# Spectral mixing, dense experts and routed experts on one core: products that follow a short chain on VectorE or ScalarE issued one unit later

## The chip, the cores and the metric

The kernel runs on one core of a Trainium2 chip. The metric is the device time of one execution in microseconds; of several runs the median counts. Engines are named as the profile names them: PE is TensorE (PEld its weight loads), DVE is VectorE, ACT is ScalarE, POOL is GpSimd, SP is SyncE, which issues most DMAs. TensorE's clock has two levels here, 1.2 and 2.4 GHz; the profile's PEclk is the share that was granted, 1.00 for the higher level and 0.5 for the lower.

## The reference

Three stages follow each other. Eight sequences of 3072 tokens with 256 channels are taken to frequencies, mixed there by a complex 256 x 256 product with a bias, shrunk towards zero, and taken back. The second stage is a dense layer, the third sends each token to the best of eight experts, of which each takes its first 768 tokens.

```python
X = np.fft.rfft(x, axis=1)                      # x: 8 x 3072 x 256
Yr = Xr @ w_r - Xi @ w_i + b_r; Yi = Xr @ w_i + Xi @ w_r + b_i
Yr = sign(Yr) * max(abs(Yr) - 0.01, 0)          # Yi likewise
x = np.fft.irfft(Yr + 1j * Yi, n=3072, axis=1).reshape(24576, 256)
r = max(x @ w_in, 0); x = (s * r * r + b) @ w_out      # 256 -> 2048 -> 256
logits = x @ w_gate; e = argmax(logits)         # 8 experts
# a token is kept if fewer than 768 tokens before it chose e
out[i] = softmax(logits)[i, e] * (max(x[i] @ w1[e], 0) @ w2[e])   # 0 if not kept
```

## The kernel before

The program order of every engine is written out by hand. The main loop goes through 8 batches of 64 **units** each, 512 units in all; a batch is a sequence, and 8 units make a **tile** i of 384 tokens. A unit is `s_unit`: four products of 384 columns on PE (line 724) for two slices of the hidden layer, a Relu on ACT (L729) and a square on DVE (L730). The squares go to routing logits; the dense layer's own output is only computed for the tokens that can need it.

Behind `s_unit`, each unit issues in this order: what `slot[k]` holds for unit k; the logit transposes `lg_fin` that are due (list `fin`); one item of the queue `todo`; and `lg_set` and `lg_out`, when a tile's logits are due (list `pend`). The slots carry the transforms of the next batch: in units 1 to 16 the first transform (`f1_mm`, one product `pz` a unit, L225), in units 22 to 50 the groups (`g_a`, `g_b`, `g_c`: products `pf`, `pmx`, `pi1`), and in units 4 and 5 of each tile the inverse (`i2_mm`, L391, copied by ACT and turned by DVE, L407, in `i2_rows`). PE, DVE and ACT each take their instructions in this order, so a product whose operand isn't there yet holds up the products of all later units.

PSUM has eight banks: two pairs for `s_unit` (`hp`), one for logits (`lp`), and three (`bgp`, by `psum()`) that all other products share.

The places that the change touches:

- **`lg_set`, `lg_out`, `lg_fin`.** Three units behind a tile's last unit, 18 products form its logits in the bank `lg`, and ACT copies them to `ls` (L760). `lg_fin` turns `ls` with four PE transposes into `plt` (L768), and DVE adds up to `LG` (L771). It comes one unit behind the copy, 64 times less four: four tiles of batch 1 have it in the same unit.
- **`decide_items`**, once for each batch: on DVE, items a, c, d and e compare bounds of the logits and count the tokens that stay open; item f counts across partitions with two small products `prt` (L864), and eight items `to_list` write lists by indirect DMAs from POOL's queue (L878). For batch b from 2 on, the queue takes them in right behind the last `lg_fin` of the batch; for batches 0 and 1 they stand behind the items of the next two points. Batch 7 has its items in the tail.
- **`xroute_items`**, once in batch 1 from its unit 51 (M = 8), once in the tail (M = 4): exact softmax and ranks. Items a and b run on DVE and ACT, c ranks by two products `prt` (L1055, L1056), d splits the rank, c2 makes the gates, and for each pair of columns e builds one-hot tables (DVE, L1108 to L1115) and f multiplies them into `ptb` (L1122).
- **`bound_items`**, in batch 0 by slots, and a second time (`diff`) in the queue behind `xroute_items` and `flags`: a makes squares and sums of weights on DVE, b fills a tile of ones, adds up across partitions with `pnr` (L691), and takes roots on ACT. `lg_set` of batch 2, unit 10, needs what it makes.
- **`load_p2`**, in batch 7, units 4 to 26, an item in every second unit: weights are loaded into `cf` buffers, copied by ACT (L1158), split by DVE (L1159) and summed on POOL (`bc`, L1161 and L1164). Then comes an empty item, and g fills a tile of ones (L1170) and multiplies (`pbc`, L1171). The buffers of `cf` are later those of `sq`, the input of the dense layer for the exact tokens.

Of the kernel before, what the change touches and what calls it, by code (L numbers as in the profile page):

```python
# [10 lines left out]
F32 = mybir.dt.float32  # L11
# [8 lines left out]
C = 256  # L20
# [20 lines left out]
NKEY = 8  # L41
# [96 lines left out]
FIRST_LAG = 13  # L138
GRAM_TO = 10
XB_AT = (2, 3, 4, 5)  # L140
WARM_F1 = 18
WARM_GROUPS = 11
MOE_CONV_AT = (0, 0, 1, 2, 3, 3, 4, 5, 6, 6, 7, 7, 8)
# [6 lines left out]
class Kern:  # L150
# [501 lines left out]
    def bound_items(self, pp, diff=False):  # L652

        nc, V = self.nc, self.nc.vector
        wb, bet = (self.wogd, self.bed) if diff else (self.wogb, self.bet)

        def own():

            v = [pp.tile([128, k], F32, tag=f"ow{n}", name="ow") for n, k in enumerate((1, E, 1, E, 1, NF))]
            mx, pr, pm, oh, bf, tf = v  # L660
            V.tensor_reduce(out=mx, in_=self.cnt, axis=AX.X, op=ALU.max)
            V.scalar_tensor_tensor(out=pr, in0=self.cnt, scalar=mx, in1=self.e8, op0=ALU.is_ge, op1=ALU.mult)
            V.tensor_reduce(out=pm, in_=pr, axis=AX.X, op=ALU.max)
            V.tensor_scalar(out=oh, in0=pr, scalar1=pm, scalar2=None, op0=ALU.is_equal)
            V.tensor_tensor(out=pr, in0=self.bw, in1=oh, op=ALU.mult)
            V.tensor_reduce(out=bf, in_=pr, axis=AX.X, op=ALU.add)
            V.tensor_scalar(out=self.cd, in0=self.cn, scalar1=bf, scalar2=1e-5, op0=ALU.subtract, op1=ALU.add)
            x = self.tq
            V.tensor_tensor(out=x, in0=self.tw, in1=oh.unsqueeze(1).to_broadcast([128, NF, E]), op=ALU.mult)
            V.tensor_reduce(out=tf, in_=x, axis=AX.X, op=ALU.add)  # L670
            V.tensor_tensor(out=self.tw, in0=self.tw, in1=tf.unsqueeze(2).to_broadcast([128, NF, E]), op=ALU.subtract)

        def a():
            tw = self.wk.tile([128, 3, NF, E], F32, tag="cl", name="tw", bufs=1)
            self.tw, self.tq, t4 = tw[:, 0], tw[:, 1], tw[:, 2]
            V.tensor_scalar(out=self.tw, in0=self.wog[:, :, 0:E], scalar1=self.ws, scalar2=None, op0=ALU.mult)
            if diff:
                own()
            V.tensor_tensor(out=self.tq, in0=self.tw, in1=self.tw, op=ALU.mult)
            V.tensor_reduce(out=self.nrm[:, 2:3], in_=self.tq.rearrange("p f e -> p (f e)"), axis=AX.X, op=ALU.add)  # L680
            V.tensor_tensor(out=t4, in0=self.tq, in1=self.tq, op=ALU.mult)
            V.tensor_reduce(out=self.nrm[:, 3:4], in_=t4.rearrange("p f e -> p (f e)"), axis=AX.X, op=ALU.add)
            V.tensor_copy(out=wb[:, :, 0:E], in_=self.tw)
            V.tensor_tensor(out=wb[:, :, 16:16 + E], in0=self.tw, in1=wb[:, :, 0:E], op=ALU.subtract)
            V.scalar_tensor_tensor(out=self.tw, in0=self.tw, scalar=-1.0, in1=self.tw, op0=ALU.mult, op1=ALU.max)

        def b():
            ones = self.wk.tile([128, 128], F32, tag="t", name="ones4", bufs=3)
            V.memset(ones, 1.0)
            pb = self.psum("pnr")  # L690
            nc.tensor.matmul(pb[:, :4], ones, self.nrm, start=True, stop=True)  # L691
            n = [pp.tile([128, k], F32, tag=f"nr{m}{diff}", name="nr") for m, k in enumerate((4, 4, 1, 1, 1, 1))]
            one, two, v, eps, x, rho = n
            nc.scalar.activation(out=one, in_=pb[:, :4], func=AF.Sqrt)
            nc.scalar.activation(out=two, in_=one, func=AF.Sqrt)
            V.tensor_scalar(out=eps, in0=two[:, 0:1], scalar1=U12, scalar2=two[:, 1:2], op0=ALU.mult, op1=ALU.add)
            V.tensor_scalar(out=eps, in0=eps, scalar1=1.05, scalar2=1e-20, op0=ALU.mult, op1=ALU.max)
            V.tensor_tensor(out=x, in0=pb[:, 2:3], in1=one[:, 0:1], op=ALU.mult)
            V.tensor_scalar(out=x, in0=x, scalar1=15.0 / (E * 512.0 * FF), scalar2=1e-30, op0=ALU.mult, op1=ALU.max)
            nc.scalar.activation(out=v, in_=x, func=AF.Sqrt)  # L700
            V.reciprocal(out=rho, in_=v)
            V.tensor_tensor(out=rho, in0=rho, in1=eps, op=ALU.mult)
            V.reciprocal(out=x, in_=rho)
            V.tensor_tensor(out=x, in0=x, in1=two[:, 3:4], op=ALU.add)
            V.tensor_tensor(out=x, in0=x, in1=eps, op=ALU.mult)
            V.tensor_tensor(out=x, in0=x, in1=eps, op=ALU.mult)
            V.tensor_scalar(out=x, in0=x, scalar1=1.1, scalar2=None, op0=ALU.mult)
            V.tensor_copy(out=bet[:, E:2 * E], in_=x.to_broadcast([128, E]))
            V.tensor_scalar(out=rho, in0=rho, scalar1=1.05, scalar2=None, op0=ALU.mult)
            V.tensor_scalar(out=self.tq, in0=self.tq, scalar1=rho, scalar2=None, op0=ALU.mult)  # L710
            V.scalar_tensor_tensor(out=wb[:, :, E:2 * E], in0=self.tw, scalar=U8, in1=self.tq, op0=ALU.mult, op1=ALU.add)
        return [a, b]


    def s_unit(self, b, i, u):
# [102 lines left out]
    def decide_items(self, b):  # L818

        nc, V = self.nc, self.nc.vector  # L820
        v = {}
# [40 lines left out]
        def f():  # L862
# [9 lines left out]
            v["x"], v["c"] = t("x", [NKEY], I32), t("c", [NKEY], I32)  # L872
            V.scalar_tensor_tensor(out=v["x"], in0=self.i128[:N1, :NKEY], scalar=off, in1=x, op0=ALU.add, op1=ALU.add)
            V.tensor_scalar(out=v["c"], in0=v["k"], scalar1=-1.0, scalar2=float(KEY + NK * b), op0=ALU.mult, op1=ALU.add)  # L874
        return [a, c, d, e, f] + [lambda n=n: self.to_list(n, v["x"], v["c"]) for n in range(NKEY)]

    def to_list(self, n, x, c):
        self.nc.gpsimd.indirect_dma_start(  # L878
# [140 lines left out]
    def xroute_items(self, M, LG, hi, lo, blk, gates, valid=None):  # L1019

        nc, V = self.nc, self.nc.vector
        v = {}
# [77 lines left out]
        n = 2  # L1100
# [18 lines left out]
        def f(k):  # L1119
            ps = self.psum("ptb")  # L1120
            for m in range(n):
                nc.tensor.matmul(ps[:, :240], v["ol"][:, m], v["rh"][:, m].rearrange("p a c -> p (a c)"),  # L1122
                                 start=(m == 0), stop=(m == n - 1))
            tv = self.T.rearrange("p a c -> p (a c)")
            V.tensor_tensor(out=tv, in0=ps[:, :240], in1=tv, op=ALU.add)
        it = [a, b, c, d, c2]
        for k in range(M // n):
            it += [lambda k=k: e(k), lambda k=k: f(k)]
        return it

    def flags(self):
# [10 lines left out]
    def load_p2(self, p2):  # L1142

        nc = self.nc
        self.wo = p2.tile([128, 2, NF, C], F32R, tag="wo", name="wo")
        bc = p2.tile([128, C], F32, tag="bc", name="bc")
        st = {}

        def load(k):
            st[k] = self.p2c.tile([128, 512], F32, tag="sq", name="cf", bufs=3)  # L1150
            nc.sync.dma_start(out=st[k], in_=self.wd[k])

        def use(k):
            if k + 2 < 8:
                load(k + 2)
            s = slice(2 * k, 2 * k + 2)
            w = st.pop(k).rearrange("p (k c) -> p k c", k=2)
            nc.scalar.copy(out=self.wo[:, 0, s], in_=w)  # L1158
            nc.vector.tensor_tensor(out=self.wo[:, 1, s], in0=w, in1=self.wo[:, 0, s].bitcast(F32), op=ALU.subtract)  # L1159
            if k == 0:  # L1160
                nc.gpsimd.tensor_tensor(out=bc, in0=w[:, 0], in1=w[:, 1], op=ALU.add)  # L1161
            else:
                for m in range(2):
                    nc.gpsimd.tensor_tensor(out=bc, in0=bc, in1=w[:, m], op=ALU.add)  # L1164
        it = [lambda: load(0), lambda: load(1)] + [lambda k=k: use(k) for k in range(8)] + [lambda: None]

        def g():
            ps = self.psum("pbc")
            ones = self.p2c.tile([128, C], F32, tag="ys", name="ones3", bufs=2)[:, :128]
            nc.vector.memset(ones, 1.0)  # L1170
            nc.tensor.matmul(ps[:, :C], ones, bc, start=True, stop=True)  # L1171
            self.yb = p2.tile([128, C], F32, tag="yb", name="yb")
            nc.vector.tensor_scalar(out=self.yb, in0=ps[:, :C], scalar1=self.wb, scalar2=None, op0=ALU.mult)
        return it + [g]

    def full_pick(self, p2):

# [522 lines left out]
    def run(self):  # L1700
        tc, nc, B = self.tc, self.nc, self.B
# [4 lines left out]
        with ExitStack() as es, tc.manual_schedule():  # L1706
# [68 lines left out]
            pend, fin, todo = [], [], []  # L1775
# [20 lines left out]
            for b in range(B):  # L1796
                slot = {}
                if b == 0:
# [6 lines left out]
                    for n, f in enumerate(gr):  # L1805
                        slot.setdefault(n * GRAM_TO // len(gr), []).append(f)
                    slot[ready].append(bi[0])
                    slot.setdefault(max(ready, GRAM_TO), []).append(bi[1])
                    slot.setdefault(20, []).append(lambda: self.route_consts(pp))
                    slot.setdefault(15, []).append(lambda: (self.load_bias1(), self.sum_mix()))  # L1810
                    slot.setdefault(40, []).append(lambda: (clear(self.list), clear(self.gd)))
# [46 lines left out]
                for k in range(64):  # L1858
# [19 lines left out]
                    while pend and pend[0][0] <= 64 * b + k:  # L1878
# [1 line left out]
                        self.lg_set(pb, pi)  # L1880
                        self.lg_out(pb, pi)
                        if pb != 1 or pi not in XB_AT:
                            fin.append((64 * b + k + 1, pb, pi))
                        else:
                            ex = exact(XB_AT.index(pi))
                            for f in ex[:4]:
# [41 lines left out]
```

## Time and profile before

| what | value |
|---|---|
| median of 3 runs (lowest to highest) | 1625.37 us (1623.62 to 1625.72) |
| the profiled execution's own time | 1614.86 us |
| its span, first to last instruction | 1612.6 us |
| mean granted clock of PE | 0.968 |
| busy: PE, DVE, ACT, POOL | 1467.8, 958.6, 814.9, 269.4 us |
| busy share: PE, DVE, ACT, POOL | 91%, 59%, 51%, 17% |

The profiled execution's own time holds 2.3 us beside its span, and it lies 10.5 us under the median of the runs. Times of the trace are counted from the span's start.

### The profile page before, as it was taken

What the parts mean: (1) busy time and instruction counts of PE and PEld (TensorE: products, weight loads), DVE (VectorE), ACT (ScalarE), POOL (GpSimd) and SP (SyncE); (2) the same over time, 40 slices, a digit from 0 to 9 for tenths busy, and PEclk for the clock granted to TensorE, in tenths of its full rate; (3) what the DMA queues carried; (4) which work ended last, traced back from release to release, by engine and by line L of the source; (5) the groups of instructions that cost most, each with busy time, mean ns of one, the idle gap of its engine ahead of it and who ended that gap; (6) DMA issues with size and microseconds to landing.
All of it is one profiled execution on the core that took longest, in us unless ns stands there. A gap on an engine that the chain in (4) does not pass through costs nothing. (4 is left out here: it accounts for less than half of the span.)

```text
span 1612.6 us, 25987 instructions
## 1 busy us (share of the span) xinstructions
PE 1467.8 (91%) x9469; PEld 1218.9 (76%) x9469; DVE 958.6 (59%) x2071; ACT 814.9 (51%) x1252; POOL 269.4 (17%) x235
## 2 busy tenths in 40 slices
PE   8997889999998799999999999999999988998984
PEld 5886678778786578868876887788778867987873
DVE  2957467545555766756765775577557776652320
ACT  2335634663334564476457546744764575652321
POOL 0634100100000040021003001300120043222020
PEclk9997999999999899999999999999999999999997
DMA  8625554663344374465446545643664447630035
GB/s 266 215 89 192 150 154 128 182 173 123 121 130 136 88 155 146 127 173 152 143 139 168 138 139 144 173 149 106 179 167 120 126 96 217 195 86 18 11 110 183
DMA packets 273843, 230.03 MB, mean 143 GB/s; under 512 B 120317, under 2 KB 228607, under 8 KB 273696
## 3 DMA queue, kind: packets, MB, share of 16 engines
q1 hardware_dynamic: 255936, 200.13, 44.8%
q10 hardware_dynamic: 13936, 25.21, 4.2%
q0 software_dynamic: 3824, 2.82, 0.7%
q8 instruction: 81, 1.33, 0.4%
q14 instruction: 66, 0.54, 0.1%
HBM read 114.18 MB, written 114.09 MB: 142 GB/s over the span
## 5 line engine op out<-in xcount | busy, mean ns | idle before, releaser
L724 PE MATMUL ph<-ah,win 128*128 128x384 f32 (+1 forms) x2048 | 488.7, 367 | 8.2 <-ACT r L729 7.8
L729 ACT ACTIVATE r<-ph 128x768 bf16<-128x768 f32 (+1 forms) x512 | 395.7, 784 | 162.8 <-PE ph L724 118.6
L730 DVE TENSOR_TENSOR qb<-r 128x768 bf16<-128x768 bf16 (+1 forms) x512 | 299.4, 586 | 281.0 <-ACT r L729 275.2
L724 PEld LDWEIGHTS ph<-ah,win 128*128 128x128 f32 x2048 | 345.1, 193 | 79.6 <-issue 40.6
L334 PE MATMUL pmx<-wm,l 128*128 128x256 f32 x1196 | 295.7, 386 | 16.9 <-DVE kb L344 9.4
L397 POOL TENSOR_TENSOR asq<-ah 128x768 bf16<-128x768 f32 x64 | 96.1, 1502 | 1040.5 <-ACT ah L393 963.9
L334 PEld LDWEIGHTS pmx<-wm,l 128*128 128x128 f32 x1196 | 221.2, 191 | 53.2 <-DVE kb L344 15.9
L391 PEld LDWEIGHTS pi<-f1t,u 96*128 96x128 f32 x1024 | 131.5, 199 | 18.7 <-issue 9.0
L391 PE MATMUL pi<-f1t,u 96*128 96x96 f32 x1024 | 136.0, 284 | 7.0 <-DVE l L261 4.3
L225 PE MATMUL pz<-x,f 96*96 96x512 f32 x240 | 126.6, 612 | 3.9 <-DMA f<-c_f 3.9
L260 ACT COPY l<-pf 128x512 f32<-128x512 f32 x84 | 49.2, 586 | 142.5 <-PE pf L252 142.1
L372 ACT COPY v<-pi 128x512 f32<-128x512 f32 x96 | 56.3, 586 | 122.7 <-PE pi L370 122.7
L370 PE MATMUL pi<-t,e 128*128 128x256 f32 x384 | 99.3, 382 | 5.2 <-DVE t L329 5.2
L252 PEld LDWEIGHTS pf<-d,zp 128*128 128x128 f32 x672 | 89.0, 194 | 11.3 <-issue 3.6
L407 DVE STREAM_TRANSPOSE at<-pi 128x384 f32<-128x384 f32 x128 | 74.1, 579 | 38.4 <-ACT ah L393 30.1
L252 PE MATMUL pf<-d,zp 128*128 128x128 f32 x672 | 90.1, 278 | 6.6 <-DMA zp<-zd 6.6
L393 ACT CAST ah<-pi 128x384 fp32r<-128x384 f32 x128 | 61.1, 479 | 59.4 <-PE pi L391 59.3
L370 PEld LDWEIGHTS pi<-t,e 128*128 128x128 f32 x384 | 72.3, 190 | 17.2 <-DVE t L329 7.0
L233 ACT COPY z<-pz 96x512 f32<-96x512 f32 x120 | 69.9, 582 | 28.4 <-PE pz L225 22.2
L878 POOL DMA_INDIRECT list<-c,x x64 | 66.7, 1043 | 56.3 <-DVE c L874 40.6
L329 DVE TENSOR_TENSOR t<-t,cl 128x512 f32<-128x512 f32 x96 | 72.2, 752 | 3.3
L760 ACT COPY ls<-lg 128x384 f32<-128x384 f32 (+1 forms) x64 | 53.2, 831 | 18.6 <-PE lg L747 16.8
(401 smaller groups left out, 1820.4 us busy)
## 6 DMA issues: line engine op xcount, KB each, us to landing
zd<-z SPq DMA_DIRECT2D x128, 192.0 KB
zp<-zd SPq DMA_DIRECT2D x96, 256.0 KB
vd<-v ACTq DMA_DIRECT2D x96, 256.0 KB
u<-vd SPq DMA_DIRECT2D x64, 384.0 KB
ad<-at SPq DMA_DIRECT2D x256, 96.0 KB
out<-zero SPq DMA_DIRECT2D x96, 256.0 KB
x<-x SPq DMA_DIRECT2D x120, 192.0 KB
sd<-stage SPq DMA_DIRECT2D x32, 256.0 KB
```

What stands on the lines that cost most here:

```text
L225: nc.tensor.matmul(o, self.f1, xs.rearrange("p a c -> p (a c)"), start=True, stop=True)
L233: nc.scalar.copy(out=z.rearrange("p a c -> p (a c)"), in_=o)
L252: nc.tensor.matmul(pv[:, h, :, gi * 64:gi * 64 + 64], zp[:, gi, h * 128:(h + 1) * 128], self.d[:, 2 * p + gi, :].rearrange("p (t m) -> p t ...
L329: nc.vector.tensor_tensor(out=t, in0=t, in1=cl, op=ALU.subtract)
L334: self.nc.tensor.matmul(o, part(h), w[:, h], start=start and h == 0, stop=stop and h == 1, skip_group_check=True)
L370: nc.tensor.matmul(ps[:, gi * C:(gi + 1) * C], self.e[:, 2 * p + gi], t[:, gi * C:(gi + 1) * C], start=True, stop=True)
L391: nc.tensor.matmul(ps[:, :TC].rearrange("p (a n) -> p a n", n=4)[:, :, n], u[:, n, h::2], self.f1t, start=True, stop=True)
L397: nc.gpsimd.tensor_tensor(out=self.asq[b, i], in0=af, in1=af, op=ALU.mult)
L407: nc.vector.transpose(out=self.ar[:, :, :, h], in_=self.at.pop((b, i, h))[:, :TC].rearrange("p (g c) -> p g c", c=32))
L724: nc.tensor.matmul(ps[:, j, :n], self.win[:, k, f], ah[:, k, t0:], start=(k == 0), stop=(k == 1))
L729: nc.scalar.activation(out=r, in_=ps[:, :, :n], func=AF.Relu)
L730: nc.vector.tensor_tensor(out=q, in0=r, in1=r, op=ALU.mult)
```

## The change

Each product named above gets one more unit between itself and the chain on DVE or ACT that it waits for. `GAP` is an empty item of the queue. `lg_fin` comes two units behind the copy, not one. `xroute_items` has c2 between b and c, and an empty item between each e and f. `decide_items` has an empty item before f, except for the last batch. `bound_items` has one between a and b, and the tile of ones is filled in a. In `load_p2` the tile of ones is filled in the item that was empty. No product, copy or DMA is added or taken away; each item of the queue still takes one unit, so that the items behind a gap come later: by 4 units behind the ranks of batch 1, by 5 behind the second `bound_items`, by 6 and 7 from item f of batches 0 and 1. `lg_fin` is moved 59 times (64 less the four and the last tile's, which the tail issues).

```diff
+GAP = [lambda: None]
     def bound_items(self, pp, diff=False):
+        st = {}
+
         def a():
+            st["ones"] = self.wk.tile([128, 128], F32, tag="t", name="ones4", bufs=3)
+            V.memset(st["ones"], 1.0)
...
         def b():
-            ones = self.wk.tile([128, 128], F32, tag="t", name="ones4", bufs=3)
-            V.memset(ones, 1.0)
             pb = self.psum("pnr")
-            nc.tensor.matmul(pb[:, :4], ones, self.nrm, start=True, stop=True)
+            nc.tensor.matmul(pb[:, :4], st["ones"], self.nrm, start=True, stop=True)
...
-        return [a, b]
+        return [a] + GAP + [b]
     def decide_items(self, b):
-        return [a, c, d, e, f] + [lambda n=n: self.to_list(n, v["x"], v["c"]) for n in range(NKEY)]
+        return [a, c, d, e] + GAP * (b < self.B - 1) + [f] + [lambda n=n: self.to_list(n, v["x"], v["c"]) for n in range(NKEY)]
     def xroute_items(self, M, LG, hi, lo, blk, gates, valid=None):
-        it = [a, b, c, d, c2]
+        it = [a, b, c2, c, d]
         for k in range(M // n):
-            it += [lambda k=k: e(k), lambda k=k: f(k)]
+            it += [lambda k=k: e(k)] + GAP + [lambda k=k: f(k)]
     def load_p2(self, p2):
-        it = [lambda: load(0), lambda: load(1)] + [lambda k=k: use(k) for k in range(8)] + [lambda: None]
+        it = [lambda: load(0), lambda: load(1)] + [lambda k=k: use(k) for k in range(8)]
+
+        def g0():
+            st["ones"] = self.p2c.tile([128, C], F32, tag="ys", name="ones3", bufs=2)[:, :128]
+            nc.vector.memset(st["ones"], 1.0)
         def g():
             ps = self.psum("pbc")
-            ones = self.p2c.tile([128, C], F32, tag="ys", name="ones3", bufs=2)[:, :128]
-            nc.vector.memset(ones, 1.0)
-            nc.tensor.matmul(ps[:, :C], ones, bc, start=True, stop=True)
+            nc.tensor.matmul(ps[:, :C], st["ones"], bc, start=True, stop=True)
-        return it + [g]
+        return it + [g0, g]
     def run(self):
-                    slot.setdefault(max(ready, GRAM_TO), []).append(bi[1])
+                    slot.setdefault(max(ready, GRAM_TO) + 1, []).append(bi[2])
...
-                            fin.append((64 * b + k + 1, pb, pi))
+                            fin.append((64 * b + k + 2, pb, pi))
```

## Rows read from the trace of the kernel before

**Rows 1.** The page's busy times, and its 40 slices (tenths) for PE and its clock.
```profile
PE 1467.8 (91%) x9469; PEld 1218.9 (76%) x9469; DVE 958.6 (59%) x2071; ACT 814.9 (51%) x1252; POOL 269.4 (17%) x235
...
PE   8997889999998799999999999999999988998984
...
PEclk9997999999999899999999999999999999999997
```
**Rows 2.** Waits of PE, whole span: us in total, times, longest.
```profile
PE prt L864 <- DVE t L859: 7.9, 8, 3.6
...
PE ptb L1122 <- DVE ol L1115: 6.7, 4, 2.4
...
PE pnr L691 <- DVE ones L689: 5.2, 2, 3.9
...
PE pi L391 <- DVE l L261: 4.3, 20, 0.2
PE plt L768 <- ACT ls L760: 4.1, 7, 2.1
...
PE pbc L1171 <- DVE ones L1170: 3.6, 1, 3.6
...
PE prt L1055 <- DVE ob L1049: 1.8, 1, 1.8
...
PE plt L768 <- POOL ls L759: 1.7, 2, 1.3
```
**Rows 3.** Waits of PE in the tail, 1436 to 1456 us.
```profile
PE plt L768 <- ACT ls L760: 0.9, 1, 0.9
...
PE prt L864 <- DVE t L859: 0.5, 1, 0.5
```
**Rows 4.** Waits of PE in batch 7, 1296 to 1350 us.
```profile
PE prt L864 <- DVE t L859: 3.6, 1, 3.6
...
PE plt L768 <- ACT ls L760: 2.1, 1, 2.1
```
**Rows 5.** Timeline of PE, two first-transform units, and four units without slots.
```profile
713.20 1.02 PE L225 MATMUL pz<-x,f 96*96 96x512 f32 x2
...
714.75 1.02 PE L225 MATMUL pz<-x,f 96*96 96x512 f32 x2
...
1297.60 1.67 PE L724 MATMUL ph<-ah,win 128*128 128x384 f32 x8 [0.20 <-ACT r L729]
1299.46 1.67 PE L724 MATMUL ph<-ah,win 128*128 128x384 f32 x8 [0.19 <-ACT r L729]
```
**Rows 6.** Stretches: us, busy (x) of PE, PEld, DVE, ACT, POOL, PEclk, DMA share, GB/s.
```profile
172.00:182.00 10.00, 8.33 (x34) 5.05 (x33) 4.95 (x21) 6.53 (x14) 0.00 (x0) 0.83 0.65 199
515.00:530.00 15.00, 10.26 (x68) 9.49 (x69) 11.88 (x46) 8.90 (x14) 1.47 (x1) 0.99 0.69 180
530.00:545.00 15.00, 10.68 (x58) 7.74 (x57) 10.78 (x31) 5.73 (x8) 1.50 (x1) 0.73 0.26 62
545.00:557.00 12.00, 8.12 (x38) 4.90 (x37) 8.93 (x43) 7.00 (x11) 0.00 (x0) 0.79 0.21 67
```
**Rows 7.** Stretches of batch 7, columns as in rows 6.
```profile
1304.00:1314.00 10.00, 6.07 (x40) 5.42 (x40) 9.52 (x33) 5.11 (x8) 3.45 (x2) 1.00 0.30 65
1314.00:1330.00 16.00, 14.76 (x101) 11.30 (x101) 13.39 (x23) 12.41 (x19) 13.25 (x13) 0.89 0.69 126
1330.00:1342.00 12.00, 8.65 (x52) 7.27 (x51) 10.30 (x15) 8.07 (x13) 11.06 (x12) 1.00 0.51 130
1342.00:1349.00 7.00, 4.18 (x27) 2.65 (x28) 2.71 (x6) 2.64 (x4) 0.62 (x1) 0.76 0.99 335
```
**Rows 8.** Waits of POOL in batch 7, 1296 to 1350 us.
```profile
POOL list L878 <- DVE c L874: 3.7, 1, 3.7
```
**Rows 9.** Timeline of ACT in batch 7: its first input for the exact tokens.
```profile
1351.75 0.62 ACT L1376 CAST ssh<-sq 128x512 fp32r<-128x512 f32 x1 [0.92 <-DMA sq<-sd]
```
**Rows 10.** Costs on DVE: the sum behind the transposes, over the whole span.
```profile
L771 DVE TENSOR_REDUCE LG<-plt x64: 673/682/691, 188.2 to 1439.4; 96x64 f32<-96x512 f32 x64
```

## The prediction

> **What bounds the kernel now.** I read the page first. PE is busy for 91% of the span, the next engine, DVE, for 59%, and nearly every slice of PE is at eight tenths or more [rows 1]. So time is lost or won where PE stands still. Away from both ends one slice stands out, the fourteenth (524 to 564 us): PE has 7 tenths and the clock 8 [rows 1], and in it lie the ranks and the second `bound_items`. Then I read the list of PE's waits, since it says which waits end in a product [rows 2]. The steps that the change touches are six of its rows: `prt` of `decide_items` 7.9 us in 8 waits, `ptb` 6.7 in 4, `pnr` 5.2 in 2, `pbc` 3.6 in one, `prt` of the ranks 1.8 in one, and `plt` 4.1 behind ACT and 1.7 behind POOL. Together that is 31.0 us, 1.9% of the span. In each of them the releaser is an instruction of a chain that was issued just ahead, in the same unit or the unit before. PE takes its products in order, so the next unit's `s_unit` stands behind each.
>
> Last I read stretches, for what the other engines do there. Around the ranks of batch 1 (515 to 557 us) DVE is busy for 11.88 + 10.78 + 8.93 = 31.6 us of 42, PE for 29.1, and the granted clock is 0.73 and 0.79 in two of three stretches [rows 6]. In batch 7 (1304 to 1349) DVE has 9.52 of 10 us, then POOL 13.25 of 16 and 11.06 of 12 [rows 7].
>
> **What a gap is worth.** A unit with a first transform lasts 1.55 us (714.75 - 713.20), one without slots 0.93 us (1299.46 - 1297.60 for two) [rows 5]. A gap lets PE do one such unit while the chain ends. It removes no instruction from any engine: what it gives is at most the wait, and at most the unit's length for one wait. Changes in the ordering of DVE's, SP's and POOL's queues come with it, and are costed where they arise.
>
> **decide_items.** Of 7.9 us, 3.6 belong to batch 7 [rows 4] and 0.5 to the tail, which gets no gap [rows 3]. The other six waits are 3.8 us, 0.63 on average. Five of them keep to first-transform units of 1.55 us, which covers them. Batch 1's moves from units 16 to 20 to units 22 to 27, among the groups, which also feed PE from DVE; I take 0.5 us off for it (from nothing to 1.0, about one of these waits). The eight list DMAs come one unit or more later in POOL's queue, which is busy for 17% of the span [rows 1] and feeds nothing near. Term: **3.3 us** (2.8 to 3.8).
>
> **Ranks and second bound_items.** The waits are 1.8 + 6.7 + 3.9 = 12.4 us (3.9 is the longest of `pnr`, and the stretch from 545 to 557 lacks 12.00 - 8.12 = 3.88 us of PE) [rows 2, 6]. With c2 between b and c the first gets a unit: 0.4 left of 1.8. An e and its f take three units where they took two, so DVE has half as long again for each: of 6.7 us I leave 1.5, though four units of 0.93 would by themselves cover only 3.7. `pnr` gets one unit of 1.55 of its 3.9: 2.35 left. Recovered: 12.4 - 0.4 - 1.5 - 2.35 = 8.2. The clock lost (1 - 0.73) x 15 + (1 - 0.79) x 12 = 6.6 us of full-speed time [rows 6], right behind waits of about 2 to 4 us; as one long wait stays in part, I give back half, 3.3. That makes 11.5, but DVE's own work limits it: in 42 us it is idle for 10.4, and the five units by which the chain is stretched, 5 x 1.55 = 7.8 us, add 41% of that (1 less DVE's 59% of the span [rows 1]), 3.2. The cap is 13.6, and chains never pack fully: **10.5 us** (5 to 13.6). Behind it: `lg_set` of batch 2, unit 10, needs b's result, now issued in unit 7, and has 3 x 1.55 = 4.7 us for it, where it had eight units. If b's chain took longer, PE would wait there for the rest. The 12 us up to 557 hold all of a and b [rows 6], and a has the greater part, so I price that at nothing and keep 1 us for it in the low bound. On SP, the store of the gates comes two units earlier, with c2; the loads behind it on that queue wait for c2's four small steps, which follow b at once, and nothing needs those loads within a unit: nothing.
>
> Here a rule speaks. The rows show the clock at 0.73 and 0.79 behind the waits and 0.99 before them [rows 6]. The Trainium skill, TensorE: Matmul & The Clock Gate, Part 1 (The HAM clock gate), says that the slow clock is the default and that steady work releases it, so that shorter pauses would cost no clock at all. By that rule this term would take all 6.6 us back and reach its cap of 13.6; by the rows, in which a wait of 2.35 us is left, half.
>
> **First bound_items.** 5.2 - 3.9 = 1.3 us of `pnr`, all covered by a later unit with a first transform, and the clock is 0.83 in these 10 us [rows 2, 6], 1.7 us lost, of which half: **2.1 us** (0.5 to 3.0).
>
> **Batch 7.** Three waits, 3.6 (`prt`), 2.1 (`plt`) [rows 4] and 3.6 (`pbc`) [rows 2], are 9.3 us, and the clock loses 0.11 x 16 + 0.24 x 7 = 3.4 [rows 7]. Most of this I don't count. DVE has no free time where `prt` waits (9.52 of 10), and POOL, which sums `bc` for `pbc`, is busy for 24.3 of 28 us behind it [rows 7]. Ones that are filled earlier help `pbc` only until `bc` is there, and the buffers that POOL frees last are those into which the exact tokens' input is loaded: ACT's first use of it waits for a DMA [rows 9]. So POOL's time sets this stretch, and what it can give is its own pause: 3.7 us in which it waits for the list's columns [rows 8], while sums that could be done stand behind. With the list two units later, the next sum comes first. **3.0 us** (0 to 9.3).
>
> **The other logit transposes.** 4.1 + 1.7 - 2.1 (batch 7) - 0.9 (tail) [rows 2 to 4] = 2.8 us in the rest, mostly fractions of a microsecond. One unit later they are behind `i2_mm`, about 2 us of products, so ACT's copy is long done; all of it is recovered. The cost is a bank: `plt` is now the third product of `psum()` in that unit, among three banks. The nearest row is `pi` waiting for a bank that DVE frees, 0.2 us each, 4.3 in 20 [rows 2]. `plt` may wait as long three times a batch, or these waits may go, since the sum of `plt` (0.68 us [rows 10]) no longer stands ahead of them on DVE. Between -4.3 and +4.3 I take nothing: **2.8 us** (-1.5 to 7).
>
> **The sum.** 3.3 + 10.5 + 2.1 + 3.0 + 2.8 = 21.7 us. The tail's two moved items cost and give nothing: PE waits for neither there. The profiled execution takes 1614.86 us, 2.3 more than its span, which would become 1593.2. It lies 10.5 us under the median of the runs shown; against that median, 1625.4 - 21.7 = **1604 us**.
>
> **Rivals.**
> - *The bank decides, and it gets slower.* Each of the 59 moved transposes holds the last free bank in the unit where the inverse is made. If the next product waited for all of the sum behind it, 0.68 us, that were 40 us, and the time 1625.4 - 18.9 + 40 = 1646. It turns the sign from 18.9 / 59 = 0.32 us a transpose. Against it: behind `plt` come `s_unit` (its own banks, 0.93 us) and often more before the next product needs one, and DVE has 41% free. 6%.
> - *The wait only moves.* DVE is what limits the ranks and batch 7; the next product waits instead, and the clock still falls. Left are 3.3, 1.3, 2.8 and some 3 us of the ranks: 1615 us. For it: 9.52 of 10 [rows 7]. Against it: 10.4 idle us of DVE around the ranks [rows 6]. 17%.
> - *The clock comes back whole.* With every pause cut, PE stays at 2.4 GHz: 3.3 + 13.6 + 3.0 + (3.0 + 3.4) + 2.8 = 29 us, so 1596 us. For it: the low clock shows only behind these waits in the middle of the span [rows 6, 7]. Against it: 2.35 us of `pnr` stay. 20%. This is what the skill's rule above would do.
> - *It does nothing that can be told*, because bank waits eat just what is won: 1625 us. 5%.
>
> **Numbers.** My forecast has 52%. What a measurement here can tell from no change is about 0.2%, 3.3 us. Faster: 52 + 20 + 17 less 1 = 88% (1 for the second rival's lower edge); same 5 + 1 = 6%; slower 6%. The low bounds give 2.8 + 4 + 0.5 + 0 - 1.5 = 5.8 us, the high ones 3.8 + 13.6 + 3.0 + 9.3 + 7 = 36.7. Both don't come together, so the range goes from 1590 to 1617; it holds the second and third rivals and leaves out the others and the far ends.
>
> **What will show it.** Right: the rows of waits for L864, L1122, L691 and L768 near zero but for one of `pnr` near 2 us, the clock over 0.9 from 530 to 545, `pbc` waiting for POOL in place of DVE. Wrong: `pi` or `pf` waiting for `LG` at L771 (the bank), or a new row of `lg` in batch 2, unit 10, waiting for `bed` or `wogd`.

## The result, and the profile after

The changed kernel takes **1603.89 us** (median of 4 runs, 1601.52 to 1608.16) against 1625.53 us of the kernel before in the same measurement (4 runs, 1623.62 to 1625.72): ratio 0.9868 (95% interval 0.9849 to 0.9887, written in square brackets from here on), 21.6 us less. The forecast was 1604. The profiled execution of the changed kernel took 1604.34 us, span 1602.1; that of the kernel before was a quick one, 10 us under the median of its runs, so I also use a second profile of the same kernel from the experiments below (span 1629.5).

The page: busy times, and the 40 slices of PE and its clock, against [rows 1].

```profile
PE 1463.2 (91%) x9469; PEld 1224.9 (76%) x9469; DVE 948.0 (59%) x2071; ACT 809.5 (51%) x1252; POOL 269.5 (17%) x235
...
PE   8996889999998899999999999999999978997985
...
PEclk9997999999999999999999999999999999998988
```

The same number of instructions and nearly the same mean clock (0.967 for 0.968; the fourteenth slice, that of the ranks, is back at nine tenths), but DVE is busy for 10.6 us less. No edit takes work from DVE; that line is the first hint that something besides PE's waits has changed.

PE's waits over the whole span, against [rows 2] (us in total, times, longest):

```profile
PE ph L727 <- ACT r L732: 11.2, 34, 2.0
PE pmx L335 <- DVE kb L345: 8.3, 11, 2.6
...
PE pbc L1176 <- POOL bc L1167: 4.9, 1, 4.9
PE pi L392 <- DVE l L262: 4.4, 20, 0.2
...
PE ptb L1125 <- DVE ol L1118: 3.5, 3, 2.1
...
PE pnr L694 <- DVE nrm L687: 2.6, 1, 2.6
...
PE prt L867 <- DVE t L862: 2.0, 2, 1.6
```

`prt` falls from 7.9 us to 2.0, `ptb` from 6.7 to 3.5, `pnr` from 5.2 to 2.6; `pbc` waits for POOL in place of DVE, and longer (4.9 for 3.6). `pi` waits for nothing of `LG`, and no `lg` waits for `bed` or `wogd`.

Stretches, against [rows 6, 7] (us; busy time of PE, PEld, DVE, ACT and POOL with instructions; granted clock; DMA). The first three hold the ranks and the second `bound_items`, the fourth what follows them, the last two batch 7 from the middle of its lists on; all begin earlier than before, so the borders are shifted.

```profile
514.00:530.00 16.00, 12.03 (x92) 10.06 (x88) 12.47 (x47) 9.78 (x15) 1.47 (x1) 0.99 0.67 178
530.00:545.00 15.00, 13.32 (x77) 9.50 (x71) 9.83 (x32) 10.06 (x13) 1.47 (x1) 0.90 0.36 92
545.00:557.00 12.00, 9.45 (x51) 7.02 (x50) 9.34 (x32) 8.68 (x14) 1.47 (x1) 1.00 0.63 174
557.00:580.00 23.00, 22.65 (x126) 15.52 (x125) 15.12 (x51) 16.08 (x25) 6.81 (x7) 0.93 0.58 148
...
1310.00:1325.00 15.00, 7.14 (x41) 5.60 (x40) 12.14 (x16) 9.14 (x14) 13.73 (x13) 1.00 0.63 175
1325.00:1332.00 7.00, 6.11 (x32) 4.35 (x33) 1.04 (x2) 1.93 (x3) 0.76 (x2) 0.52 1.07 346
```

**Where the time went.** To place the gain I cut each trace at the start of the first `lg` product of a tile (tiles are numbered through, 8 to a batch; the `lg` of tile 15 ends batch 1). The table is worked out from PE's records of those products; us per stretch. Kernels other than the first three are the experiments told below.

```
                   start-2   2-14  14-15  15-20  20-55  55-63    end    span
kernel before        210.0  321.0   22.1  108.2  641.0  133.7  176.7  1612.6
  again              214.3  320.2   22.0  109.6  644.7  138.7  179.8  1629.5
changed kernel       209.0  320.1   13.1  113.3  627.2  137.0  182.2  1602.1
fin_only             209.6  319.0   22.8  108.9  629.6  137.4  182.7  1610.0
ranks_only           210.9  320.7   13.8  117.3  644.0  137.0  184.5  1628.2
decide_only          212.9  320.1   22.0  107.8  646.2  134.4  181.5  1624.8
all_but_fin          206.8  320.5   13.0  112.6  637.8  134.8  182.0  1607.6
nosq_before          207.2  321.1   21.0  105.6  633.2  134.6  176.1  1598.8
nosq_after           207.1  317.1   12.2  108.0  625.2  134.2  178.5  1582.3
```

Against the mean of the two profiles of before, the changed kernel is 3.2 us shorter up to tile 2, 4.6 from 14 to 20 (the ranks: 9 won, half given back), **15.7 from 20 to 55**, where no ranks and no list of batch 7 are, and 0.8 and 4.0 longer behind. Start, batch 7 and end differ by 3 to 5 us between executions of one kernel, and the changed kernel lies within that or near it. The gain sits in the ordinary tiles, where my sum had about 6 us.

The length of an ordinary tile shows it without that scatter: the mean time from the `lg` of tile p of a batch to that of the next tile, over tiles 20 to 55.

```
p                       0      1      2      3      4      5      6      7
kernel before       14.16  18.35  27.58  27.58  22.49  12.26   9.82  16.86
  again             15.01  18.42  27.59  27.58  22.50  12.26   9.82  16.86
changed kernel      14.12  17.92  27.23  27.23  22.15  11.81   9.49  15.99
fin_only            14.15  17.80  27.24  27.23  22.15  11.93   9.49  16.53
decide_only         15.28  19.36  27.58  27.59  22.49  12.26   9.82  16.02
all_but_fin         14.17  18.37  27.58  27.58  22.49  12.27   9.82  16.02
sum_twice_before    14.41  18.37  27.84  27.84  22.75  12.26   9.83  16.86
nosq_before         14.17  17.90  27.22  27.21  22.12  12.25   9.82  16.57
nosq_after          14.12  17.60  27.19  27.19  22.10  11.81   9.47  15.98
delay_after         14.39  17.87  27.28  27.28  22.23  11.81   9.47  15.98
```

### The profile page after: what moved, and what is told of

Same layout as the page of the kernel before. It is cut to its first block, busy times and chain, and to the rows that moved or that the text cites. A ratio compares the mean times of both kernels' runs of the same rounds, so it can differ in the third digit from the quotient of the medians.

```text
span 1602.1 us, 25976 instructions
## 1 busy us (share of the span) xinstructions
PE 1463.2 (91%) x9469; PEld 1224.9 (76%) x9469; DVE 948.0 (59%) x2071; ACT 809.5 (51%) x1252; POOL 269.5 (17%) x235
## 5 line engine op out<-in xcount | busy, mean ns | idle before, releaser
L733 DVE TENSOR_TENSOR qb<-r 128x768 bf16<-128x768 bf16 (+1 forms) x512 | 284.7, 558 | 265.4 <-ACT r L732 251.9
L261 ACT COPY l<-pf 128x512 f32<-128x512 f32 x84 | 49.3, 587 | 135.4 <-PE pf L253 133.7
```

What stands on the lines that cost most here:

```text
L733: nc.vector.tensor_tensor(out=q, in0=r, in1=r, op=ALU.mult)
```

## The experiments

Twelve kernels ran, in three groups of four; in each group the kernel before ran beside them on the same chip (1632.0, 1625.6 and 1618.4 us), so ratios are compared, not times. Where a difference in us is given behind a ratio, it is the ratio taken on the kernel before of that group. Line numbers move by a few between kernels.

**The scatter of the kernel before: before_again.** No edit.

> The kernel before, unchanged, profiled once more and timed against itself. The profiled execution of before lay 10.5 us under the median of its runs, so the two traces at hand differ by 10.5 us and the medians by 21.6. If that execution was a rare quick one, this trace has a span near 1621 to 1624 and shows where such an execution saves 10 us (I expect the tail from 1438 us on, where the changed kernel seems to lose 5.5 us, and batch 2, where it seems to give back 5). If instead 1614 is as common as 1625, the times of the rounds scatter between the two and the true gain is nearer to 10 us than to 21.

1631.49 us (12 runs), ratio 0.9994 [0.998, 1.0009]. The tables above show where executions of one kernel differ: at the start, in tile p = 0, in batch 7 and at the end, and hardly in the tiles p = 1 to 7.

**The transposes alone: fin_only.**

```diff
-                            fin.append((64 * b + k + 1, pb, pi))
+                            fin.append((64 * b + k + 2, pb, pi))
```

> Only the logit transposes come one unit later; no gap anywhere else. By the prediction's term (2.8 us, from -1.5 to 7) the time falls by about 3 us. By the comparison of the two traces it falls by 10 to 14 us: each tile between the groups is 0.34 us shorter, which is not the wait of the transposes for ACT but the wait of the mixing product pmx for kb on DVE, 27 us later in order, ahead of which the sum of plt no longer stands. By the rival that the bank decides, it is no faster or slower.

1613.9 us, ratio 0.9879 [0.9858, 0.99]: 19.7 us less. That is more than the 10 to 14 us that the two traces had led me to expect. The edit that I had priced at 2.8 us gives nearly as much as the whole change; every tile but p = 0 is 0.33 us or more shorter.

**decide_items alone: decide_only.** Only the `GAP` before f.

> Only the empty item ahead of the counts in decide_items. By the prediction's term 3.3 us (2.8 to 3.8) plus what batch 7 gives: 3 to 5 us faster. If POOL decides batch 7 (its lists come later, so that the sums that free the load buffers come later too), that batch gives nothing or loses up to 3 us, and the whole is between 0 and 4 us faster.

1624.68 us, ratio 0.9949 [0.9926, 0.9972]: 8.3 us less (4.6 to 12.1), more than the 3 to 5 expected. In the trace the tile with the count (p = 7) is 0.84 us shorter, 16.02 for 16.86, a little more than the 0.63 of the prediction. In this execution the next two tiles are longer (15.28 and 19.36), with `plt` waiting for `ls`; all_but_fin has the same edit and does not show that (14.17, 18.37), so I do not hold it against the edit. What the runs gain beyond the 0.84 us of each count is not placed by this trace.

**The ranks alone: ranks_only.** Only c2 ahead of c, and the `GAP` between e and f.

> Only the ranks: c2 between b and c, and an empty item between e and f. By the prediction's share of its term (8.5 us of waits less 1.9 left, and half of 4 us of clock) 7 to 9 us faster. If the wait only moves to what follows in batch 2, 2 to 4 us. The tail has the same items and should not change by more than 1 us either way.

1629.31 us, ratio 0.9974 [0.9957, 0.999]: 4.2 us less (1.6 to 7.0), where 7 to 9 were expected and 2 to 4 if the wait only moves. The stretch from tile 14 to 15 falls by 8 us as in the full change, and the next one grows by nearly as much (117.3 for 108.2 and 109.6). PE's waits from 515 to 600 us name the place:

```profile
PE pnr L692 <- DVE ones L690: 5.3, 1, 5.3
PE ptb L1123 <- DVE ol L1116: 4.1, 3, 2.1
PE pmx L335 <- DVE l L266: 2.5, 1, 2.5
```

The second `bound_items` still fills its ones and multiplies at once, now later and longer (5.3; 3.9 before). Without its own gap, what the ranks win is lost there. So `ranks` and `bound_items` belong together, as the prediction had costed them.

**All but the transposes: all_but_fin.** The changed kernel with `k + 1` in `fin`.

> The changed kernel with the logit transposes back at one unit behind the copy; all its other edits stand. Theory (the transposes carry nearly the whole gain): 1.0 to 0.4% under the kernel before at most, that is 6 to 13 us less, and if the other edits' waits only move, 0 to 6 us less. Rival (the gains add up as the prediction summed them, 18.9 us without the transposes): 17 to 20 us less than the kernel before, ratio about 0.988.

1609.97 us, ratio 0.9909 [0.9886, 0.9932]: 14.8 us less (11.1 to 18.5). The 18.9 that the prediction gave to these edits is just beyond the interval, and the 6 to 13 of the theory reach into it. By runs the two halves, 19.7 and 14.8, make more than the whole, 21.5; the tables place 13 us of fin_only from tile 20 to 55 and 5 us of all_but_fin there and 5 in the ranks. What overlaps beyond that I cannot tell from scatter of the start and the end.

**Is it the sum on DVE? sum_twice_before, sum_twice_after.** My first theory was that `LG` (0.68 us on DVE) stood ahead of `kb`, for which `pmx` waits.

```diff
             in_=ps[:N1].rearrange("p (n j x) -> p n x j", n=4, j=8), axis=AX.X, op=ALU.add)
+        dup = self.rp.tile([N1, 4, 2 * E], F32, tag="dup", name="dup", bufs=1)
+        nc.vector.tensor_reduce(out=dup, in_=ps[:N1].rearrange("p (n j x) -> p n x j", n=4, j=8), axis=AX.X, op=ALU.add)
```

> The kernel before, in which DVE forms each tile's sum of plt (0.68 us) twice, the second time into a scratch tile that nothing reads. Theory (order on DVE): in the kernel before this sum stands ahead of kb on DVE in the unit where the groups' pmx waits for kb, so each of some 30 tiles with groups becomes longer by between half of 0.68 us and all of it: +10 to +20 us, with the wait of pmx for kb longer by that much. Rival (only the wait of plt for ls counts, the sum is hidden): nothing comes behind the sum, 0 to +3 us.

> The changed kernel with the same doubled sum. Theory (order on DVE): the sum now stands behind kb, in a unit where DVE has time left, so doubling it costs much less than in the kernel before: 0 to +5 us against the changed kernel (about 1604 to 1610 us where the kernel before takes 1630). Rival (DVE's total work counts, wherever it stands): as much as in the kernel before, 0.3 to 0.7 us a tile, +18 to +40 us for both.

1629.25 us, ratio 1.0027 [1.0009, 1.0045], 4.4 us more; and 1602.82 us, ratio 0.9866 [0.9836, 0.9895], none more than the changed kernel. The theory falls: it asked for 10 to 20 us, and the wait of `pmx` for `kb` did not grow (9.4 us in 20; 1.1 the longest, as before). What the second sum does in the kernel before is hold the bank: `pi` of the inverse waits for it and ends 0.25 us later, and each such tile is 0.25 us longer (27.84 for 27.58). The row of PE's waits:

```profile
PE pi L391 <- DVE dup L775: 4.3, 11, 0.7
```

**What follows the transposes.** I then laid one tile of both kernels side by side (tile 27, p = 3; timeline of PE, ACT, POOL and DVE: start, us, engine, line, operation, in brackets the idle time before it). The kernel before, in its second profile:

```profile
792.63 0.60 PE L768 MATMUL plt<-ident,ls 128*96 128x128 f32 x4
...
797.68 1.18 PE L391 MATMUL pi<-f1t,u 96*128 96x96 f32 x8 [0.22 <-DVE l L261]
...
798.90 0.48 ACT L393 CAST ah<-pi 128x384 fp32r<-128x384 f32 x1 [0.87 <-PE pi L391]
...
799.52 1.47 POOL L397 TENSOR_TENSOR asq<-ah 128x768 bf16<-128x768 f32 x1 [26.11 <-ACT ah L393]
...
800.48 0.93 DVE L730 TENSOR_TENSOR qb<-r 128x768 bf16<-128x768 bf16 x1 [1.82 <-ACT r L729]
...
805.31 0.41 DVE L344 TENSOR_TENSOR kb<-pmx,bias 128x256 f32<-128x256 f32 x1
...
805.78 0.48 PE L334 MATMUL pmx<-wm,l 128*128 128x256 f32 x1 [0.19 <-DVE kb L344]
```

The changed kernel:

```profile
782.69 1.18 PE L392 MATMUL pi<-f1t,u 96*128 96x96 f32 x8 [0.22 <-DVE l L262]
...
783.72 0.64 PE L771 MATMUL plt<-ident,ls 128*96 128x128 f32 x4
...
783.91 0.48 ACT L394 CAST ah<-pi 128x384 fp32r<-128x384 f32 x1 [0.87 <-PE pi L392]
...
784.53 1.47 POOL L398 TENSOR_TENSOR asq<-ah 128x768 bf16<-128x768 f32 x1 [25.77 <-ACT ah L394]
...
785.94 0.56 DVE L733 TENSOR_TENSOR qb<-r 128x768 bf16<-128x768 bf16 x1 [0.86 <-ACT r L732]
...
790.40 0.41 DVE L345 TENSOR_TENSOR kb<-pmx,bias 128x256 f32<-128x256 f32 x1
...
790.89 0.90 PE L335 MATMUL pmx<-wm,l 128*128 128x256 f32 x3
```

In the kernel before, `plt` stands ahead of `pi`. So `pi`, ACT's copy `ah` and POOL's square `asq` come later, and `asq` (799.52 to 800.99) is still running when DVE starts `qb` at 800.48. That `qb` takes 0.93 us and ends 0.42 us behind POOL. Its backlog makes `kb` late, and `pmx` waits 0.19. With `plt` behind `pi`, `asq` ends at 786.00, `qb` starts at 785.94, takes 0.56, and the wait is gone. This one wait is the whole difference between the two tiles: the `ph` ahead of that `pmx` starts 15.46 us behind the tile's `lg` in the first profile of before and 15.48 in the changed kernel, `pmx` itself at 16.59 and 16.26. The 0.33 us are the idle 0.2 and most of the overlap with the product ahead, which is lost too. In the second profile of before 57 of the 512 `qb` take over 0.7 us; 50 of them start under a running square and end 0.41 to 0.42 us after it (0.28 in the narrower ones of batch 0). In the changed kernel 20 take over 0.7 us, 12 of them under a square. The lines of `qb` (busy us, mean ns, then idle time before), the kernel before again, changed, and nosq_before below, one fence each:

```profile
L730 DVE TENSOR_TENSOR qb<-r 128x768 bf16<-128x768 bf16 (+1 forms) x512 | 300.7, 588 | 286.3 <-ACT r L729 257.6 <-issue 16.3 <-ACT z L233 6.0
```

```profile
L733 DVE TENSOR_TENSOR qb<-r 128x768 bf16<-128x768 bf16 (+1 forms) x512 | 284.7, 558 | 265.4 <-ACT r L732 251.9 <-issue 4.1 <-ACT z L234 3.5
```

```profile
L730 DVE TENSOR_TENSOR qb<-r 128x768 bf16<-128x768 bf16 (+1 forms) x512 | 278.0, 544 | 297.9 <-ACT r L729 291.1
```

**Without the square: nosq_before, nosq_after.** POOL fills `asq` with zeros, so the bias term that the logits take from these squares is left out.

```diff
-            nc.gpsimd.tensor_tensor(out=self.asq[b, i], in0=af, in1=af, op=ALU.mult)
+            nc.gpsimd.memset(self.asq[b, i], 0.0)
```

> The kernel before without POOL's square asq of each tile's input: POOL fills asq with zeros instead, and reads nothing for it, so the bias term of the logits that comes from these squares is left out. Theory (DVE's qb waits for POOL): in the trace of before 58 of the squares qb start while POOL makes asq and end 0.41 us after it, 0.93 us where others take 0.56, 21 us in all, and a good third to two thirds of that reaches PE through kb. Without the square no qb is long, the wait of pmx for kb in the tiles with groups goes, and the time falls by 8 to 18 us though the transposes stay where they were. Rival (the place of the transposes counts by itself, in PE's or DVE's order): 0 to 3 us less, and pmx waits for kb as before.

> The changed kernel with the same edit, zeros in place of the square. Theory (DVE's qb waits for POOL): only 5.8 us of long qb are left there (10 of them, against 21 us in the kernel before), so 0 to 5 us less than the changed kernel, 1599 to 1604 us where the kernel before takes 1625, and nosq_before comes near to it but for what the other edits give. Rival (POOL's work counts wherever it lies): as much less as nosq_before, 8 to 18 us.

nosq_before: 1601.68 us, ratio 0.9904 [0.9889, 0.9918], 15.5 us less with the transposes where they were. Its tiles p = 1 to 4 are as short as those of the changed kernel (27.22 and 27.23), and with both edits they gain hardly more (27.19). Two edits that do not add up remove the same thing: POOL's square in front of `qb`. (Tile p = 1 differs: each edit gains there 0.4 to 0.6 us alone, and both together 0.8.) PE's wait for `kb` falls as the theory asked, from 13 waits to 5 in tiles 20 to 55, in nosq_before, in fin_only and in the changed kernel alike; over the whole span, the kernel before again, then nosq_before:

```profile
PE pmx L334 <- DVE kb L344: 9.4, 20, 1.1
```

```profile
PE pmx L334 <- DVE kb L344: 4.8, 7, 0.7
```

The tiles p = 5 and 6 show the other half: there nosq_before gains nothing (12.25, 9.82), and the moved transposes gain 0.33. It is their own wait: in tile 29 (p = 5) the first `plt` stands idle 0.19 us for `ls` in the kernel before, 0.20 in nosq_before, and not at all in the changed kernel.

nosq_after: 1585.34 us, ratio 0.9801 [0.9786, 0.9815], 10.8 us under the ratio of the changed kernel, where 0 to 5 were expected. In tiles 20 to 55 only 2.0 us come from it; 6.2 lie from 14 to 20 and 3.0 from 2 to 14 (against delay_after, on the same chip, it is 10.4 by runs). So the square costs more around the ranks than its long `qb` show. Part of it can be placed. The square holds up other operations of DVE as well: in the changed kernel `pr` (L1048) takes 1.25 us under a square and 0.23 in nosq_after, where PE's wait of 1.1 us of `prt` behind it falls to 0.04; and `full` (L1138), a small step ahead of the second `bound_items`, takes 1.07 us for 0.16, and `pnr` then waits 2.6 us for 1.7. The changed kernel:

```profile
549.27 1.47 POOL L398 TENSOR_TENSOR asq<-ah 128x768 bf16<-128x768 f32 x1 [17.26 <-ACT ah L394]
...
549.70 1.07 DVE L1138 TENSOR_SCALAR full<-cnt 128x8 f32<-128x8 f32 x1
```

nosq_after:

```profile
543.83 0.16 DVE L1138 TENSOR_SCALAR full<-cnt 128x8 f32<-128x8 f32 x1
```

Of the 6.2 us from 14 to 20, some 2.6 are a wait of `pmx` for `kb` at 623 us that stands in the changed kernel's profile and in no other, so it cannot be laid to the square; and the mean clock there is 0.973 and 0.986, at most 1.7 us of full-speed time. The rest stays open.

**The square a little later: delay_after.** The changed kernel, with a copy of 16 columns on POOL ahead of the square.

```diff
+            dly = self.mo.tile([128, 16], F32, tag="dly", name="dly", bufs=1)
+            nc.gpsimd.tensor_copy(out=dly, in_=af[:, 1, 0:16])
             nc.gpsimd.tensor_tensor(out=self.asq[b, i], in0=af, in1=af, op=ALU.mult)
```

> The changed kernel with one more small copy on POOL, 16 columns of ah, ahead of each square, which delays the square by some 0.5 us and computes nothing that is used. Theory (DVE's qb waits for POOL): the square again ends behind the start of qb in the tiles with groups, qb there takes 0.9 us or more, pmx waits for kb again, and 8 to 20 us of the gain are lost, with the transposes where the change puts them. Rival (the place of the transposes counts by itself): 0 to 2 us slower.

1595.77 us, ratio 0.9871 [0.985, 0.9892], no slower than the changed kernel. The expectation had the delay wrong: the copy takes 0.21 us, not 0.5, and against the tile's `lg` the square ends 0.13 us later.

```profile
L399 POOL COPY dly<-ah 128x16 f32<-128x16 f32 x64 | 13.6, 213 | 996.9 <-ACT ah L394 996.9
```

`qb` is then 0.06 us longer (0.62) and the tile 0.05 (27.28 for 27.23): the direction is the theory's, but a delay as long as the wait was not tried.

**Batch 7: list6_early.** The changed kernel with `GAP * (b < self.B - 2)` in `decide_items`.

> The changed kernel with no empty item before f in the decide_items of batch 6, whose items run in batch 7; all else stands. Theory (the list's DMAs now stand between the sums of bc on POOL's queue and keep cf buffers back): with the lists two units earlier as in the kernel before, ACT's waits in the copies of wo shrink, pbc waits less than 4.9 us, and 1 to 3 us are won in batch 7, while prt L867 waits there again for up to 3.6 us, so that the sum is -2 to +2 us. Rival (the position of the list does not matter, batch 7 is bound by POOL's sums alone): pbc waits 4.9 us as before and the returned wait of prt adds up to 3.6 us.

1601.67 us, ratio 0.9869 [0.9839, 0.9898]: as the changed kernel. `prt` waits 3.6 us there again, `pbc` 3.3 in place of 4.9, and ACT's copies of `wo` wait 1.6 us for `cf` in place of 3.7. POOL's waits in batch 7, changed kernel:

```profile
POOL bc L1167 <- DMA cf<-wd: 6.8, 1, 6.8
```

and list6_early:

```profile
POOL list L881 <- DMA cf<-wd: 7.1, 1, 7.1
```

In both, POOL's long idle time ends with a load of `cf`, and the second sum starts no sooner with the list ahead: 7.5 us behind the first in the kernel before again, 7.8 in the changed kernel, 9.2 in list6_early. So the list does not set the start of the sums. The shorter waits of `pbc` and of ACT's copies are what the theory asked for, but 1.6 and 2.1 us are less than batch 7 differs by from one execution of a kernel to the next, so whether the lists keep the later buffers back is not decided.

**A version to beat it: sqact_late.** list6_early, with `pbc` two units later, and the square of tiles 0 to 5 of each batch on ACT, one unit behind the inverse.

```diff
-            nc.gpsimd.tensor_tensor(out=self.asq[b, i], in0=af, in1=af, op=ALU.mult)
+            if i > 5:
+                nc.gpsimd.tensor_tensor(out=self.asq[b, i], in0=af, in1=af, op=ALU.mult)
...
+            if i < 6:
+                nc.scalar.activation(out=self.asq[b, i], in_=self.aT[b, i].bitcast(F32), func=AF.Square)
...
-        return it + [g0, g]
+        return it + [g0, lambda: None, lambda: None, g]
```

> A version that should beat the changed kernel: tiles 0 to 5 of each batch make the square on ACT, in the unit behind the inverse, instead of on POOL; the decide_items of batch 6 have no empty item before f; and pbc comes two units later. Theory (DVE's qb waits for POOL; pbc waits for POOL's sums): the long qb that are left go, pbc waits for 0 to 2 us in place of 4.9, and the time is 2 to 7 us under the changed kernel, if ACT's 0.8 us a tile finds room between r. Rival (ACT has no room): ph waits for r by 0.3 to 0.8 us in each of 48 tiles, and it is 5 to 20 us slower than the changed kernel.

1593.42 us, ratio 0.9849 [0.9835, 0.9863], the lowest of the complete kernels. On the same chip delay_after took 1595.8, and the intervals overlap, so it is not shown to beat the changed kernel. The tiles p = 2 and 3 are at 27.18, so ACT has room for the square there; p = 1 and 6 are longer than in the changed kernel (18.10 and 9.85 for 17.92 and 9.49), and from tile 20 to 55 the kernel takes 630.2 us for 627.2. `pbc`, for which 0 to 2 us were expected, got worse:

```profile
PE pbc L1179 <- DVE at L409: 6.4, 1, 6.4
```

## Why the prediction was right, and where it was not

The sum was right, 21.7 us for 21.6, and it was right through errors against each other: the logit transposes gave far more than their term, the ranks and batch 7 less. That the sum comes so near is luck. (Its 1593.2 us is the profiled execution's own time less 21.7; the span would be 1590.9.)

- **The other logit transposes: the step that was mis-sized.** 2.8 us forecast (-1.5 to 7); fin_only alone gives 19.7 (16.3 to 23.2), and from all_but_fin to the changed kernel the ratios give 6.7; in tiles 20 to 55 it is 13 us by fin_only and 11 from all_but_fin to the changed kernel. Two things were missed. First, PE's own row of waits [rows 2] was too small a measure. In the traces a matmul starts some 0.16 us before the end of the one ahead (in tile 27 above, `plt` at 783.72 and the end of `pi` at 783.87), so a late `plt` shows as a wait only when that overlap is used up. What an engine's idle time ended with, for the line of `plt`, matmuls and weight loads together, says more, though one wait can count in both (18.2 us in 38 in the profile that I predicted from); the kernel before again, then the changed one:

```profile
its engine sat idle before it (us, times) until:
  ACT ls L760: 28.9, 45
```

```profile
its engine sat idle before it (us, times) until:
  ACT ls L763: 4.3, 6
```

  Second, I asked what bank `plt` takes in its new unit and not what moves up in its old one. `pi`, `ah` and `asq` move up, and with them DVE's `qb`.
- **decide_items**, 3.3 us forecast: 0.84 us a batch at p = 7, 16.86 to 16.02, where 0.63 was taken. Right in mechanism, a little low; the 8.3 us that decide_only gives by runs are more than these counts explain.
- **Ranks and second bound_items**, 10.5 forecast (5 to 13.6): 4.6 in the stretch from 14 to 20, and 5 to 8 in the profiles of all_but_fin, sum_twice_after, delay_after and list6_early. Left are 1.1 of `prt`, 3.5 of `ptb` and 2.6 of `pnr`, for 0.4, 1.5 and 2.35. The waits lost 5.2 us where I had 8.2; the largest miss is `ptb`, to which I gave half as long again for each e and f. And half of what the ranks won was given back behind them, which the term did not count. The clock came back as far as forecast: 0.99, 0.90 and 1.00, and 0.93 behind (1.00 there before), is 0.2 + 1.5 + 1.6 = 3.3 us lost of 6.6.
- **The rule on the clock.** The Trainium skill, TensorE: Matmul & The Clock Gate, Part 1 (The HAM clock gate), states that the slow clock is the default and that activity releases it; by that, the prediction noted, all 6.6 us would come back. No run here bears that out or refutes it: waits of 2.1 and 2.6 us remain, and the granted clock behind them is 0.90 and 0.93.
- **First bound_items**, 2.1 forecast: not shown. Its wait is gone (one `pnr` is left of two), but the start of fin_only, which does not have the edit, is as short (209.6) as that of the changed kernel (209.0).
- **Batch 7**, 3.0 forecast: nothing, 137.0 us from 55 to 63 for 133.7 and 138.7. The step that failed is POOL's pause of 3.7 us [rows 8] as time to be had: with the list out of the way the next sum still needs a load of `cf`, and POOL now waits 6.8 us for that.
- **Rivals.** The bank did not decide: nothing waits for `LG`. But sum_twice_before shows that it is near, since 0.68 us more on the bank make `pi` wait. That waits only move was true of the ranks alone (ranks_only); in the whole change 4.4 of the 9 us that the ranks won were given back behind them. The clock did not come back whole: the span's mean is 0.967.

## What to carry to other kernels

When a product is moved behind others in an engine's order, follow what moves up in its place, across all engines, as far as the next wait; here that was worth more than the wait the move was made for. Read idle time of matmuls and weight loads together, and count the overlap that a late product loses, before a wait is called small, and test a suspected cause with two edits that should remove the same thing: if they give 0.35 and 0.37 us a tile alone and 0.39 together, it is one thing. Gaps in one chain can be lost at the next chain that has none, so put them in together.

## What the runs showed of the hardware

An operation of DVE that reads two inputs from SBUF did not run beside POOL's square, which reads SBUF. `qb`, 0.56 us by itself, started under `asq` 58 times in the second profile of the kernel before. Where it had to wait (50 of them took over 0.7 us) it ended 0.41 us behind the end of `asq`, however late that was (0.28 for the narrower `qb` of batch 0), so that it took 0.93 us, in some tiles 1.2 to 1.6. The trace shows this as busy time of DVE and not as a wait. The Trainium skill, SBUF — State Buffer, Who interferes with whom, states that a DVE instruction with two SBUF inputs contends with a GpSimd instruction that reads SBUF, and not with one that only writes it. The traces agree with both halves. In nosq_after POOL only writes, and a `qb` that starts 0.54 us before the end of the fill takes its usual time (timeline of POOL and DVE):

```profile
813.43 0.74 POOL L398 MEMSET asq<- 128x768 bf16 x1 [21.36 <-PE lg L750]
...
813.63 0.56 DVE L733 TENSOR_TENSOR qb<-r 128x768 bf16<-128x768 bf16 x1 [2.04 <-ACT r L732]
```

The fill ends at 814.17, `qb` at 814.19, as if POOL had not been there; under the square, a `qb` that started as early took 0.93 us. Operations of DVE with one input are not all free of it: `full` above, a TENSOR_SCALAR of 128 x 8, took 1.07 us under the square for 0.16, while the sum `nrm` (a TENSOR_REDUCE) that started under one took its usual 0.69.
